# The first four units' key blocks of v are issued by GpSimd in its own queue, not by SyncE

## The chip, the cores and the metric

The kernel runs on one core of a Trainium2 chip. The metric is the device time of one execution in microseconds (us). TensorE is called PE, VectorE DVE, ScalarE ACT, GpSimd POOL and SyncE SP, as the profile does.

## What is computed

An attention over 2 batches, 8 heads, 768 positions and 64 dimensions, in float32, and behind it two dense layers of expert form. A query sees the keys less than 16 positions away, and besides one summary per block of 32 positions (the maximum of the block's keys, the mean of its values).

```
scores_l = scale * q @ k.T            # kept where |i - j| < 16
scores_s = scale * q @ k_sum.T + log(32)
a = softmax(concat(scores_l, scores_s))
x = a @ concat(v, v_sum)              # to [1536, 512]
x = relu(x @ w_in) ** 2 @ w_out       # 512 -> 2048 -> 512
h = x @ w_in2
out = (h * sigmoid(1.702 * h)) @ w_out2
```

## The kernel before

The 1536 tokens are twelve units of 128, units 0 to 5 in the first batch. For a unit, `scores` multiplies q by the keys of its two half windows and by the 24 summaries, and DVE adds the mask and finds the row's extreme (line 750). `softmax` takes the exponentials on ACT (line 765), adds a small number to the sums (line 769, here on POOL), inverts them on DVE (line 779) and multiplies (line 772, on DVE or on POOL). `tail` transposes the result on PE (line 802) and multiplies it by v (line 814). It then splits the product into a high and a low part, `xh` and `xl` (line 827), which the first layer's matmuls read (line 998). All matmuls of the layers are done three times, on high and low parts, to keep float32 accuracy.

For the product with v each unit has a tile `vw`: for each of its two halves (c = 0, 1) 96 rows of v around the half, the key block, and 24 rows of summaries. `load_vw` brings the key blocks with one DMA per half (line 509). A key block of 96 positions and 8 heads is 768 pieces of 64 numbers, 256 bytes each; the very first block has 80 positions, as the window begins before the text does. There are four such tiles (`vw_ring`). The summary rows are put into two of them by copies (line 521) and into the other two by DMAs that POOL issues (line 531).

The summaries of v need the whole of v: three loads of 512 KB into `kin` buffers (`load_long`, line 474, and `load_short`, line 481), whose blocks PE averages (line 576) before DVE and ACT copy the result to `vs` (line 364). There are three `kin` buffers, and the loads of k use them as well.

The order of the work is planned by the program before the kernel exists. A string of items, ORDER, names the steps of the attention (`v,0` is `load_vw(0)`, `h` a head step, `t` a tail, `w` the preparation of a weight block) in the order in which they are placed. `Plan.op` gives each step a start time from costs written beside it, and all steps are emitted by start time, so that each engine has one fixed list and works through it in order. `plan.dma` places a DMA on SP. `plan.fill` adds matmuls on the identity (line 1774, "warm") where PE would stand idle. DMAs of SP share eight semaphores in turn, so an issue can wait for the DMA eight before it.

```
def dma(self, moves, fn, reads=(), writes=()):
    return self.op("SP", 0.0, fn, reads, writes, moves=moves)
```

Of the kernel before, what the change touches and what calls it, by code (L numbers as in the profile page):

```python
# [39 lines left out]
LAST = (2,), (0, 1), (3,)  # L40
SHAKE = (14, 0.15)
WARM = (15.52, 6), (21.24, 5)
KEPT = 10
LOW3 = 7.4999 / 2.0 ** 32
LESS = 99.0
# [97 lines left out]
class Plan:  # L143
# [37 lines left out]
    def op(self, eng, dur, fn, reads=(), writes=(), after=(), port=False, moves=0.0):  # L181
        ready = self._ready(eng, self._deps(reads, writes, after)) + self._shaken()
        assert not any(b.dead for b, _ in (*reads, *writes))
        o = Op()
        o.eng, o.fn, o.seq, o.far = eng, fn, len(self.ops), eng == "SP"
        if eng == "SP":
            o.start = self._place(("SP",), max(ready, 0.8), self.ISSUE)
            self._take("SP", o.start, self.ISSUE)
            t = self._place(("DMA",), o.start + self.FLIGHT, moves)
            if t > o.start + self.FLIGHT:  # L190
                self.busy["SP"].remove((o.start, o.start + self.ISSUE))
                o.start = self._place(("SP",), t - self.FLIGHT, self.ISSUE)
                self._take("SP", o.start, self.ISSUE)
                t = self._place(("DMA",), o.start + self.FLIGHT, moves)
            self._take("DMA", t, moves)
            o.end = t + moves + self.LAND
        else:
            lines = (eng, "PORT") if port else (eng,)
            o.start = self._place(lines, ready, dur)
            for e in lines:  # L200
                self._take(e, o.start, dur)
            o.end = o.start + dur
        self.ops.append(o)
        for b, key in reads:
            b.ops.append(o)
            b.readers.setdefault(key, []).append(o)
        for b, key in writes:
            b.ops.append(o)
            b.writer[key] = o
            b.readers[key] = []  # L210
        return o
# [96 lines left out]
def kernel(  # L308
# [11 lines left out]
    nc = tc.nc  # L320
# [38 lines left out]
    plan = Plan()  # L359
# [135 lines left out]
    def load_vw(i):  # L495
        b, j = divmod(i, NB)
        assert vw_ring.k == i
        buf = vw_ring.take()
        rows = vs_rows[i % NV]
        for c in range(2):  # L500
            r0 = NSUM * (1 - c)
            s0 = j * P + c * HALF - EDGE
            lo, hi = max(s0, 0), min(s0 + WIN, S)
            if s0 < 0:
                op("POOL", 0.46, lambda c=c: nc.gpsimd.memset(buf.t[0:HALF, c, :], 0.0),
                   writes=[(buf, (c, "w")), (rows, c)])
            if s0 + WIN > S:
                op("POOL", 0.46, lambda c=c: nc.gpsimd.memset(buf.t[HALF:WIN, c, :], 0.0), writes=[(buf, (c, "w"))])
            plan.dma(1.0, lambda c=c, r0=r0, s0=s0, lo=lo, hi=hi: nc.sync.dma_start(
                out=buf.t[r0 + lo - s0:r0 + hi - s0, c, :].rearrange("p (h d) -> p h d", h=H),  # L510
                in_=v[b, :, lo:hi, :].rearrange("h p d -> p h d")), writes=[(buf, (c, "w"))])
        vw[i] = buf
# [1191 lines left out]
    def drain():  # L1704
        while pending:
            finish()

    todo = dict(
        K=load_kl, B=load_ks, T=t_kp, V=sum_v0, g=head_half, q=load_q, k=load_k, v=load_vw, tk=t_k, tq=t_q,
        h=head, t=tail, ps=put_vs, pk=put_ks, sv=sum_v, w=lambda f, z: prep(0, f, f % RING, (z,)),  # L1710
        m=lambda i: op("POOL", 1.6, lambda: make_mask(i), writes=[(consts, ("mask", i))]),
# [15 lines left out]
    if 0 in TWICE:  # L1727
        firsts = [int(item.split(",")[1]) for item in ORDER.split() if item[:2] == "w," and item[-2:] == ",0"]
        to_save.update({f for _, f in keep_w}, [f for f in firsts[::-1] if (0, f) not in keep_w][:KEPT])
    attn_ops = []  # L1730
# [44 lines left out]

    plan.fill(0.27, keep_warm, first_ops["acc3"], WARM)
    with tc.manual_schedule():
# [30 lines left out]
```

## Time and profile before

| | |
|---|---|
| median of 3 runs | 567.93 us (567.53 to 568.5) |
| the profiled execution | 568.08 us, span 566.4 us |
| PE busy | 560.2 us, 99% of the span |
| DVE, ACT, POOL busy | 495.6, 412.7, 41.8 us |
| granted TensorE clock | 1.00 |
| DMA | 120.26 MB, mean 212 GB/s |
| queue of SP (hardware), queue of POOL (software) | 104416 and 192 packets |

The profile is of one execution; its span is what the trace covers, and the 1.7 us between it and the time lie around it. Issuing a DMA is not counted as busy. A DMA has an issue on the engine that starts it, with a duration of its own, and a landing, counted from the issue until its semaphore is complete. A wait is put down to the event that came last.

### The profile page before, as it was taken

What the parts mean: (1) busy time and instruction counts of PE and PEld (TensorE: products, weight loads), DVE (VectorE), ACT (ScalarE), POOL (GpSimd) and SP (SyncE); (2) the same over time, 40 slices, a digit from 0 to 9 for tenths busy, and PEclk for the clock granted to TensorE, in tenths of its full rate; (3) what the DMA queues carried; (4) which work ended last, traced back from release to release, by engine and by line L of the source; (5) the groups of instructions that cost most, each with busy time, mean ns of one, the idle gap of its engine ahead of it and who ended that gap; (6) DMA issues with size and microseconds to landing.
All of it is one profiled execution on the core that took longest, in us unless ns stands there. A gap on an engine that the chain in (4) does not pass through costs nothing.

```text
span 566.4 us, 11027 instructions
## 1 busy us (share of the span) xinstructions
PE 560.2 (99%) x3838; PEld 481.3 (85%) x3838; DVE 495.6 (88%) x1110; ACT 412.7 (73%) x899; POOL 41.8 (7%) x112
## 2 busy tenths in 40 slices
PE   8999999999999999999999999999999999999997
PEld 8889988888878887888888888888888888899997
DVE  4788898888889899989999899998999999789974
ACT  4899889898896668777789757477366676677650
POOL 6143311211100000000000000000000000000000
PEclk9999999999999999999999999999999999999999
DMA  9999999886677864545558657576255555686723
GB/s 273 247 270 281 273 267 302 262 216 198 208 238 259 269 221 148 182 152 168 186 181 282 206 168 235 185 241 199 92 203 187 176 200 191 213 286 205 222 90 112
DMA packets 104663, 120.26 MB, mean 212 GB/s; under 512 B 28736, under 2 KB 72512, under 8 KB 104608
## 3 DMA queue, kind: packets, MB, share of 16 engines
q1 hardware_dynamic: 104416, 119.17, 67.1%
q0 software_dynamic: 192, 0.39, 0.4%
q8 instruction: 30, 0.49, 0.4%
q14 instruction: 25, 0.20, 0.1%
HBM read 86.64 MB, written 32.51 MB: 210 GB/s over the span
## 4 chain that ended last, share of the span: by engine, by line
PE 94%; SPq 1%; DMA 1%; DVE 1%; ACT 1%; issue 0%; DVEq 0%; ACTq 0%
PE acc L1440 14%; PE m L1440 12%; PE h L998 10%; PE acc L1053 8%; PE acc L1347 8%; PE acc L1345 7%; PE m L1345 5%; PE acc L998 5%; PE m L1347 4%; PE m L1055 4%; PE acc L1055 3%; PE h L1347 2%; PE h L1345 2%; PE m L802 2%; PE m L814 2%; PE m L998 1%
## 5 line engine op out<-in xcount | busy, mean ns | idle before, releaser
L963 DVE TENSOR_TENSOR w<-xw,w 128x512 fp32r<-128x512 f32 (+1 forms) x141 | 83.9, 609 | 2.7 <-ACT w L958 2.0
L958 ACT CAST w<-xw 128x512 fp32r<-128x512 f32 (+1 forms) x127 | 68.5, 552 | 23.0 <-DVE xw L932 15.9
L998 PE MATMUL h<-xh,w 128*128 128x512 f32 (+1 forms) x184 | 55.6, 364 | 0.0
L1440 PE MATMUL m<-top,w 128*128 128x512 f32 x210 | 53.5, 391 | 0.1
L932 DVE SCALAR_TENSOR_TENSOR xw<-raw,xw 128x512 uint32<-128x512 uint32 x67 | 45.8, 689 | 4.6 <-ACT raw L923 2.7
L923 ACT ACTIVATE raw<-raw 128x512 f32<-128x512 f32 x72 | 47.7, 679 | 1.0 <-DMA raw<-in_moe_w_in_dram 0.8
L1440 PEld LDWEIGHTS m<-top,w 128*128 128x128 f32 x210 | 38.7, 188 | 8.2 <-ACT r L363 0.5
L1440 PE MATMUL acc<-top,w 128*128 128x512 f32 x174 | 43.9, 390 | 0.0
L1053 PE MATMUL acc<-gh,w 128*128 128x512 f32 (+1 forms) x160 | 42.6, 353 | 0.0
L1440 PE MATMUL acc<-xh,w 128*128 128x512 f32 x124 | 42.1, 389 | 0.0
L1440 PEld LDWEIGHTS acc<-top,w 128*128 128x128 f32 x174 | 32.4, 188 | 6.5
L998 PEld LDWEIGHTS h<-xh,w 128*128 128x128 f32 x184 | 33.1, 189 | 5.6 <-issue 1.0
L765 ACT ACTIVATE sm<-sm,st 128x120 f32<-128x120 f32 x96 | 36.6, 385 | 0.2
L927 DVE TENSOR_SCALAR xw<-raw 128x512 uint32<-128x512 uint32 x67 | 29.1, 438 | 6.8 <-DMA raw<-in_moe_w_in_dram 5.4
L998 PE MATMUL h<-xl,w 128*128 128x512 f32 (+1 forms) x92 | 32.5, 353 | 0.0
L958 ACT CAST top<-gs 128x512 fp32r<-128x512 f32 x38 | 23.5, 618 | 11.3 <-DVE gs L947 3.0
L1053 PEld LDWEIGHTS acc<-gh,w 128*128 128x128 f32 x160 | 27.7, 189 | 4.4 <-issue 0.3
L963 DVE TENSOR_TENSOR top<-gs,top 128x512 fp32r<-128x512 f32 x41 | 27.9, 685 | 2.8 <-ACT top L958 2.6
L1347 PE MATMUL acc<-w,gh 128*128 128x256 f32 x136 | 28.0, 283 | 0.0
L1053 PE MATMUL acc<-gl,w 128*128 128x512 f32 (+1 forms) x80 | 27.8, 348 | 0.0
L1440 PEld LDWEIGHTS acc<-xh,w 128*128 128x128 f32 x124 | 23.3, 188 | 4.8
L998 PE MATMUL acc<-xh,w 128*128 128x512 f32 x80 | 26.1, 389 | 0.0
(300 smaller groups left out, 1501.6 us busy)
## 6 DMA issues: line engine op xcount, KB each, us to landing
raw<-in_moe_w_in_dram SPq DMA_DIRECT2D x36, 512.0 KB, 4.7
raw<-in_moe_w_out_dram SPq DMA_DIRECT2D x36, 512.0 KB, 4.6
w<-xw SPq DMA_DIRECT2D x50, 256.0 KB, 2.3
xw<-w SPq DMA_DIRECT2D x27, 256.0 KB, 2.8
w<-w SPq DMA_DIRECT2D x24, 256.0 KB, 2.8
r<-g SPq DMA_DIRECT2D x17, 256.0 KB, 3.7
vw<-in_v_dram SPq DMA_DIRECT2D x20, 192.0 KB, 4.7
g<-w SPq DMA_DIRECT2D x14, 256.0 KB, 2.0
```

The lines of the kernel that those rows point to most:

```text
L765: nc.scalar.activation(out=s.t[:, h, :], in_=s.t[:, h, :], func=AF.Exp, bias=st.t[:, 0, h:h + 1], scale=-1.0, accum_out=st.t[:, 1, h:h + 1])
L923: nc.scalar.activation(out=top, in_=top, func=AF.Prelu, scale=-(2.0 ** -80), alpha=-(2.0 ** -32))
L927: plan.soonest([("DVE", 0.36, True, lambda: nc.vector.tensor_scalar(out=x.t, in0=raw.t[:, :, 0], scalar1=29, scalar2=None, op0=ALU.logical ...
L932: op("DVE", 0.64, lambda: nc.vector.scalar_tensor_tensor(out=x.t, in0=raw.t[:, :, 1], scalar=3, in1=x.t, op0=ALU.logical_shift_left, op1=A ...
L958: plan.soonest([("ACT", 0.09 + 0.44 * fr, False, lambda: nc.scalar.copy(out=hi.t[:, hc], in_=src())), ("DVE", 0.05 + 0.4 * fr, True, lambd ...
L963: eng.tensor_tensor(out=lo.t[:, lc], in0=src(), in1=hi.t[:, hc].bitcast(F32), op=ALU.subtract)
L998: nc.tensor.matmul(hp.t[:, cols], lhsT=w.t[:, kc * P:(kc + 1) * P], rhs=x.t[:, kc, cols], start=(kc == 0 and n == 0), stop=(kc == KC - 1 a ...
L1053: nc.tensor.matmul(a.t[:, cols], lhsT=w.t[:, j * P:(j + 1) * P], rhs=g.t[:, cols], **st)
L1055: nc.tensor.matmul(a.t, lhsT=g.t[:, j * P:(j + 1) * P], rhs=w.t, **st)
L1345: nc.tensor.matmul(b.t, lhsT=w.t[:, x + j * P:x + j * P + P], rhs=g.t, **st)
L1347: nc.tensor.matmul(b.t[:, (j % 2) * CH:(j % 2) * CH + CH], lhsT=g.t[:, j * P:j * P + P], rhs=w.t[:, x:x + CH], **st)
L1440: nc.tensor.matmul(bank.t, lhsT=a, rhs=rhs(b, kh), start=(begin and k == 0 and n == 0), stop=(k == 1 and n == 2), skip_group_check=True)
```

## The change

A tuple names four units, and for them `load_vw` calls `dma_start` of GpSimd in place of that of SyncE. The plan is the same: it still counts the DMA as one of SP's, so start times and every other step stay, and the eight calls now stand in POOL's list at the places that their planned times give.

```
+BESIDE = 0, 1, 2, 3
...
+            queue = nc.gpsimd if i in BESIDE else nc.sync
-            plan.dma(1.0, lambda c=c, r0=r0, s0=s0, lo=lo, hi=hi: nc.sync.dma_start(
+            plan.dma(1.0, lambda c=c, r0=r0, s0=s0, lo=lo, hi=hi, queue=queue: queue.dma_start(
                 out=buf.t[r0 + lo - s0:r0 + hi - s0, c, :].rearrange("p (h d) -> p h d", h=H),
                 in_=v[b, :, lo:hi, :].rearrange("h p d -> p h d")), writes=[(buf, (c, "w"))])
```

The lines behind the first are one later in the changed kernel, and those from line 509 on two: line 509 becomes 511, 769 becomes 771. The lists of PE, DVE and ACT do not change.

POOL before, from the last of the copies that fill the windows of k's first units to the steps of unit 3's softmax (`st` and `sm` are the sums and the scores of a softmax):

```order
L662 COPY kw<-kw 128x5x16
L769 TENSOR_SCALAR st_344<-st_344 128x4
L769 TENSOR_SCALAR st_391<-st_391 128x4
L769 TENSOR_SCALAR st_344<-st_344 128x4
L521 COPY vw<-vs_451 24x512
...
L772 TENSOR_TENSOR sm_519<-sm_519,st_520 128x480
L678 MEMSET kw 128x4x16
L769 TENSOR_SCALAR st_520<-st_520 128x4
```

and the same stretch of POOL in the changed kernel:

```order
L664 COPY kw<-kw 128x5x16
L511 DMA vw<-in_v_dram 80x8x64
L511 DMA vw<-in_v_dram 96x8x64 x2
L771 TENSOR_SCALAR st_344<-st_344 128x4
L511 DMA vw<-in_v_dram 96x8x64 x2
L771 TENSOR_SCALAR st_391<-st_391 128x4
L511 DMA vw<-in_v_dram 96x8x64
L771 TENSOR_SCALAR st_344<-st_344 128x4
L523 COPY vw<-vs_451 24x512
...
L774 TENSOR_TENSOR sm_519<-sm_519,st_520 128x480
L511 DMA vw<-in_v_dram 96x8x64
L680 MEMSET kw 128x4x16
L511 DMA vw<-in_v_dram 96x8x64
L771 TENSOR_SCALAR st_520<-st_520 128x4
```

Six of the eight issues stand around the first two softmax steps, and two ahead of the sixth, that of unit 3's second half.

SP before, from the last loads of v for the summaries on (`kin_470` and `kin_526` are loads of k, `raw` a weight block):

```order
L481 DMA kin_339<-in_v_dram 128x8x128
L509 DMA vw<-in_v_dram 80x8x64
L509 DMA vw<-in_v_dram 96x8x64 x5
L449 DMA kin_470<-in_k_dram 128x4x128 x2
L449 DMA kin_526<-in_k_dram 128x4x128
L918 DMA raw_557<-in_moe_w_out_dram 128x1024
L449 DMA kin_526<-in_k_dram 128x4x128
L509 DMA vw<-in_v_dram 96x8x64 x2
L918 DMA raw_656<-in_moe_w_out_dram 128x1024
```

and in the changed kernel:

```order
L482 DMA kin_339<-in_v_dram 128x8x128
L450 DMA kin_470<-in_k_dram 128x4x128 x2
L450 DMA kin_526<-in_k_dram 128x4x128
L920 DMA raw_557<-in_moe_w_out_dram 128x1024
L450 DMA kin_526<-in_k_dram 128x4x128
L920 DMA raw_656<-in_moe_w_out_dram 128x1024
```

The loads of k now follow the last load of v directly; unit 4's key block is the first that SP still issues.

## Rows read from the trace of the kernel before

**Rows 1.** The page, part 1: busy us (share) and instructions of each engine.

```profile
PE 560.2 (99%) x3838; PEld 481.3 (85%) x3838; DVE 495.6 (88%) x1110; ACT 412.7 (73%) x899; POOL 41.8 (7%) x112
```

**Rows 2.** Windows: us, busy PE, PEld, DVE, ACT, POOL, clock, DMA share, GB/s.

```profile
15.00:20.00 5.00, 4.36 (x80) 3.95 (x76) 4.18 (x17) 3.98 (x10) 0.00 (x0) 1.00 1.11 332
...
50.00:170.00 120.00, 120.00 (x1085) 100.92 (x1083) 102.33 (x302) 105.74 (x277) 20.96 (x36) 1.00 0.83 248
```

**Rows 3.** The chain that ended last, 0 to 50: start us, us, what.

```profile
9.44 7.63 DMA qin<-in_q_dram
...
21.19 1.06 PE m L576 x16
...
24.19 0.28 DVE vs L364
...
30.27 0.65 PE m L802 x4
...
34.73 1.63 PE h L998 x12
...
41.48 1.08 PE acc L814 x32
```

**Rows 4.** Timeline, PE's weight loads: start us, us, what, [idle before <-releaser].

```profile
21.18 0.79 PEld L576 LDWEIGHTS m<-kin,band 128*24 128x24 f32 x16 [0.31 <-DMA kin<-in_v_dram]
```

**Rows 5.** Timeline of SP's DMA issues, first 60 us.

```profile
12.75 1.21 SPq L474 DMA_DIRECT2D kin<-in_v_dram  x2
...
15.20 9.23 SPq L509 DMA_DIRECT2D vw<-in_v_dram  x6
24.53 1.58 SPq L449 DMA_DIRECT2D kin<-in_k_dram  x3
...
27.91 1.91 SPq L509 DMA_DIRECT2D vw<-in_v_dram  x2
```

**Rows 6.** DMA queues, 19.6 to 21.2 us: packets, MB, share of 16 engines.

```profile
DMA packets 1017, 0.30 MB, mean 186 GB/s; under 512 B 879, under 2 KB 1017, under 8 KB 1017
...
q1 hardware_dynamic: 1017, 0.30, 99.1%
```

**Rows 7.** Timeline of POOL, first 60 us.

```profile
13.44 0.26 POOL L662 COPY kw<-kw 128x80 f32<-128x80 f32 x1
21.46 0.23 POOL L769 TENSOR_SCALAR st<-st 128x4 f32<-128x4 f32 x1 [7.77 <-ACT sm L765]
22.96 0.22 POOL L769 TENSOR_SCALAR st<-st 128x4 f32<-128x4 f32 x1 [1.28 <-ACT sm L765]
24.48 0.22 POOL L769 TENSOR_SCALAR st<-st 128x4 f32<-128x4 f32 x1 [1.29 <-ACT sm L765]
...
31.46 0.99 POOL L772 TENSOR_TENSOR sm<-sm,st 128x480 f32<-128x480 f32 x1 [0.17 <-DVE st L779]
...
33.16 0.22 POOL L769 TENSOR_SCALAR st<-st 128x4 f32<-128x4 f32 x1 [0.61 <-ACT sm L765]
```

**Rows 8.** Line 531, DMAs that POOL issues already: ns min/median/max, and landing.

```profile
L531 POOL DMA_DIRECT2D vw<-vs x4: 592/638/802, 25.9 to 101.8; - x4
...
DMA to landing us min/median/max: 4.1/5.6/7.4
```

**Rows 9.** Timeline of DVE, first 60 us.

```profile
24.19 0.28 DVE L364 COPY vs<-m 24x128 f32<-24x128 f32 x1 [1.53 <-PE m L576]
24.40 0.15 DVE L779 RECIPROCAL st<-st 128x4 f32<-128x4 f32 x1
...
25.64 0.17 DVE L779 RECIPROCAL st<-st 128x4 f32<-128x4 f32 x1
...
33.61 0.17 DVE L779 RECIPROCAL st<-st 128x4 f32<-128x4 f32 x1
33.70 0.66 DVE L827 TENSOR_TENSOR xl<-acc,xh 128x512 fp32r<-128x512 f32 x1
```

**Rows 10.** Timeline of PE, first 60 us: first use of xl.

```profile
34.89 0.28 PE L998 MATMUL h<-xl,w 128*128 128x256 f32 x1
```

## Prediction

> **What bounds the kernel now.** Read the engines' busy times first [rows 1]: TensorE is busy for 560.2 of 566.4 us. Then read stretches [rows 2]: from 50 to 170 us PE has no idle time at all, from 15 to 20 us it has 0.64 us. So nothing later in the run can be shortened by a change of queue, and little of a delay can be made up there. What the change can move is the moment at which PE comes into steady work. The chain of waits gives that moment [rows 3]: up to 17.1 us it hangs on the q load that was issued at 9.44 us, then on PE, then on v's sums on PE (line 576), which the copy of vs on DVE waits for at 24.19 us, then on DVE, and from 30.27 us on it stays on PE. At 34.73 us the first matmuls of the MoE layer start. A delay that still exists there goes to the end one for one.
>
> Two details decide. The second group of the v sums starts at 21.18 us behind a wait of 0.31 us for a v load [rows 4]; this is the place at which a slower load costs at once. And the softmax steps of line 769 on POOL feed DVE's reciprocals with little room [rows 7, 9]: the second ends at 23.18 and its reciprocal starts at 24.40, the third ends at 24.70 and is used at 25.64, the sixth ends at 33.38 and is used at 33.61.
>
> **What is removed from SP.** Eight issues go: six that hold SP from 15.20 to 24.43 us and two from 27.91 to 29.82 us [rows 5]. The k loads behind them now wait for the kin buffer that the first v sums read, free at about 21.2 us [rows 3], so they leave some 3.2 us sooner than at 24.53. I count this as nothing: what covers it is PE's and DVE's own order between 24 and 35 us, where the chain shows no load [rows 3]. If the cover failed it could only show in DVE's idle 1.53 us before the copy of vs [rows 9].
>
> **What is added on POOL.** Eight issues of 256-byte pieces: 640 pieces in the first, 768 in each other one. Three stand behind the copy that ends at 13.70, two between the first and the second softmax step, one between the second and third, two between the normalisation that ends at 32.45 and the sixth step [rows 7]. How long POOL needs for one, call it g, is not in the trace: the nearest rows are POOL's four issues of vs, 48 pieces each, median 0.638 us [rows 8]. Below, g is 0.64 if the number of pieces costs nothing; above it is 16 times that, 10.2 us, if every piece costs the same. I take 1.8 us: 1017 packets in 1.6 us at 99.1% of 16 engines are 25 ns per packet and engine [rows 6], so one such DMA (48 packets per engine) drains in 1.2 us, and I let the issue go at that pace on top of its 0.6. That lies near the lower row, since a regular pattern should not pay a full issue per piece. The Trainium skill, "DMA: Bandwidth & Descriptors", Anatomy of one DMA — SWDGE, goes further down: many descriptors can be emitted before their cost shows. By that sentence g is 0.64 and the sum below is 2.2 us; no run here shows it yet.
>
> Term 1, the transfers. Before, vw's packets stood behind the v loads in SP's queue. Now the first three DMAs are in a queue of their own from 13.70 us, beside the v loads issued from 12.75 us [rows 5], while the engines have no room (share 1.11 from 15 to 20 us [rows 2]). Their 2176 packets are 136 per engine, or 3.4 us at 25 ns. Bounds: 0 (they drain behind the v loads as before) to 3.4 us (all go ahead of the second v load). With g of 1.8 us the third is issued at 19.1 us, too late to get ahead; the first two are 88 packets per engine, **2.2 us**. The wait at 21.18 us has no slack, so they count in full. A delay of the q load that lands at 17.1 us by the first DMA (40 packets, at most 1.0 us) lies on the same chain ahead of it and is inside the 2.2. What speaks against is that POOL's own vs DMA took up to 7.4 us to land, against 4.1 at best [rows 8]: its queue gives way, too. The Trainium skill has in the same page, Queues, rings and completion order, that an engine goes round robin between queues packet by packet; by it the term would be the full 3.4 us, and the 7.4 us, where three packets per engine waited among SP's, fits that badly.
>
> Term 2, POOL's steps between 21 and 26 us. The first step may slip 0.5 us with the q load, to 22.2; two DMAs to 25.8; second step to 26.0; one DMA to 27.8; third step ends 28.0. With term 1 its reciprocal is due at 25.64 + 2.2 = 27.8. So **0.2 us** of it shows, nothing if g is below 1.7.
>
> Term 3, the last two issues. With 2.4 us of delay the normalisation ends at 34.85; two DMAs to 38.45; the sixth step ends at 38.7, and its reciprocal was due at 33.61 + 2.4 = 36.0. That is 2.7 late. Behind it stands line 827 on DVE, which ends at 34.36 and is first read at 34.89 [rows 9, 10]: 0.5 us of room. **2.2 us** remain. The key blocks themselves are just in time: with the longest landing, 7.4 us [rows 8], they are there at 45.9, and the tail that reads them, at 41.48 in the chain [rows 3], has slipped to 46.1.
>
> **Sum:** 2.2 + 0.2 + 2.2 = 4.6 us. The profiled execution took 568.08, within 0.15 of the median 567.93; from the median this gives **572.5 us**. Both ends of the terms: 0 transfers and g of 0.64 give 568 (two issues then take 1.3 us against 0.7 of gap before the sixth step, covered by 0.2 + 0.5 of room); above, it is open, see the second rival.
>
> **Rivals.** (a) *Nothing shows*: SP's queue keeps its share and g is near 0.64; 568.0. For it: the 7.4 us of landing [rows 8] and POOL's emptiness from 13.70 to 21.46 us [rows 7]. Against it: no slack at 21.18. (b) *POOL becomes the bound*: g is 3 us or more. Then the first three end at 22.7, the first step at 22.9, two more 28.9, second step 29.1, one 32.1, third step 32.4 against 25.64: 6.7 late. The normalisation ends at 39.2, two more 45.2, the sixth step 45.4 against 33.61: 11.8 late, less 0.5, so 579.2 us; above 2.5 us each further us of g adds 8. For it: 768 pieces against 48. Against it: nothing but the floor. (c) *Faster*: SP, free 3.2 us sooner, and a v load with no vw pieces crowding its tail let the third v sum end sooner. The chain then shortens by the idle time before the copy of vs, at most 1.53 us [rows 9]: 566.4. It decides when the v loads land more than 1.1 us sooner than now; the only wait for them that shows is 0.31 us [rows 4], which speaks against. (d) *It does nothing*: the listing shows the eight issues on POOL, so this has 1 in 100 and is held in (a).
>
> **Chances.** Measured times of this kernel differ by up to 0.2% without a cause, 1.1 us: no change is 566.8 to 569.1. Forecast (569.1 to 577) 0.56; (a) 0.18; (b) above 577, 0.20; (c) 0.06. So faster 0.06, no change 0.18, slower 0.76. The range leaves out about 0.04 below 567.4 and 0.13 above 580.0, where g passes 3 us. The forecast's own range is 569.1 to 577.
>
> **What would show it.** Right: line 511 on POOL in rows of 1.5 to 2.2 us; the second group of line 576 starting near 23.4 us; the third softmax step on POOL behind a DMA and not behind ACT; the first MoE matmul near 39.3 us; PE without idle afterwards. Wrong: rows of 0.6 to 0.8 us with line 576 unmoved (a); rows of 3 us and more with DVE's reciprocals waiting for POOL in every unit (b); the copy of vs before 23 us (c). A clock below 1.00 in the opening, where PE would now idle longer than before, would add a cost that no row here prices. If the delay at 34.7 us were not found again at the end, the first paragraph's reading would be wrong.

## The result and the profile after

The changed kernel takes **570.67 us** (median of 6 runs, 570.23 to 572.04) against 567.73 us before (6 runs in the same comparison, 567.38 to 568.62): ratio 1.0053, 95% interval 1.0039 to 1.0067. It is slower by 2.9 us; forecast were 572.5 us and a range of 567.4 to 580.0. The profiled execution took 570.4 us with a span of 568.6, 2.2 us more than before.

Part 1 of the page, busy us by engine, answers to [rows 1]. POOL has eight instructions and 7.4 us more; the eight issues, which are counted here, make 6.5 of them:

```profile
PE 559.6 (98%) x3838; PEld 481.0 (85%) x3838; DVE 496.7 (87%) x1110; ACT 412.6 (73%) x899; POOL 49.2 (9%) x120
```

The windows, with columns as in [rows 2]:

```profile
15.00:20.00 5.00, 5.00 (x97) 4.55 (x98) 4.89 (x25) 4.58 (x15) 2.53 (x3) 1.00 1.14 345
20.00:25.00 5.00, 2.12 (x28) 1.72 (x20) 1.39 (x8) 3.33 (x18) 3.04 (x6) 1.00 1.13 220
...
50.00:170.00 120.00, 120.00 (x1116) 101.48 (x1115) 102.71 (x302) 105.25 (x277) 21.82 (x36) 1.00 0.84 247
```

The same stretch of the opening in the kernel before, which [rows 2] leave out:

```profile
20.00:25.00 5.00, 4.96 (x85) 3.91 (x78) 3.16 (x21) 4.88 (x26) 0.67 (x3) 1.00 0.72 150
```

The steady part is as it was, and the loss stands in the opening: from 20 to 25 us PE works for 2.12 us of 5, where it worked for 4.96. The clock is at 2.4 GHz throughout in this execution. The chain that ended last, start us, us, what:

```profile
13.69 11.31 DMA kin<-in_v_dram
25.00 0.04 issue
25.04 0.68 PE m L578 x16
25.72 0.02 issue
25.75 0.28 DVE vs L365
...
31.83 0.65 PE m L804 x4
...
34.43 0.60 issue
35.03 0.34 PE acc L816 x4
...
37.12 1.62 PE h L1000 x12
```

Set against [rows 3], the copy of vs is 1.56 us later (25.75 against 24.19), the transpose behind it still 1.56 (31.83 against 30.27), and the first MoE matmul 2.39 (37.12 against 34.73). In between stands a second loss: PE waits 0.60 us in the middle of the second product with v, and nothing that the profile shows releases it ("issue"); the product is 0.83 us longer in all. The 2.39 us are found again at the end as 2.2.

The chain begins with the *third* v load, issued at 13.69 us and landed after 11.31. PE's timeline says the same, with the idle time and its releaser in brackets:

```profile
19.02 1.79 PE L578 MATMUL m<-kin,band 128*24 128x128 f32 x32
25.04 0.64 PE L578 MATMUL m<-kin,band 128*24 128x128 f32 x16 [2.92 <-DMA kin<-in_v_dram]
```

The first two v sums run without a break, where [rows 4] had a wait of 0.31 us before the second; it is the third that waits. SP's queue (answering to [rows 5]) and POOL's timeline ([rows 7]):

```profile
20.12 1.47 SPq L450 DMA_DIRECT2D kin<-in_k_dram  x3
21.69 0.48 SPq L920 DMA_DIRECT2D raw<-in_moe_w_out_dram  x1
```

```profile
15.16 2.53 POOL L511 DMA_DIRECT2D vw<-in_v_dram  x3 [1.82 <-issue]
20.40 0.22 POOL L771 TENSOR_SCALAR st<-st 128x4 f32<-128x4 f32 x1 [2.71 <-ACT sm L767]
20.68 1.58 POOL L511 DMA_DIRECT2D vw<-in_v_dram  x2
22.33 0.22 POOL L771 TENSOR_SCALAR st<-st 128x4 f32<-128x4 f32 x1
22.60 0.81 POOL L511 DMA_DIRECT2D vw<-in_v_dram  x1
23.48 0.22 POOL L771 TENSOR_SCALAR st<-st 128x4 f32<-128x4 f32 x1
```

```profile
L511 POOL DMA_DIRECT2D vw<-in_v_dram x8: 776/807/947, 15.2 to 34.9; - x8
```

POOL's issue of 768 pieces takes 0.81 us (ns min/median/max in the last row), against 0.638 for 48 pieces [rows 8]: sixteen times the pieces cost 0.17 us. SP's k loads leave 4.4 us sooner. What the engines carry from 20 to 22 us is in the view of DMA queues (packets, MB, share of 16 engines):

```profile
q0 software_dynamic: 128, 0.38, 101.6%
q1 hardware_dynamic: 59, 0.03, 8.7%
```

[rows 6] had SP's queue alone there. POOL's queue moves packets of 4096 bytes (sixteen of the 256-byte pieces in one); the third v load goes in packets of 512 bytes. A landing is sixteen increments of a semaphore, so it has sixteen parts, presumably one for each DMA engine. The trace's semaphore events give, for the third v load:

| run | 8th part, us | 15th part | 16th part (landing) |
|---|---|---|---|
| before | 20.31 | 21.68 | 22.80 |
| change | 20.34 | 22.30 | 25.00 |

The 8th part is no later, and none of the first fifteen is more than 0.8 us later. The last part lags already before the change, and under POOL's packets it loses 2.2 us more.

### The profile page after: what moved, and what is told of

Read it like the earlier page. It is cut to its first block, busy times and chain, and to the rows that moved or that the text cites. A ratio compares the mean times of both kernels' runs of the same rounds, so it can differ in the third digit from the quotient of the medians.

```text
span 568.6 us, 11033 instructions
## 1 busy us (share of the span) xinstructions
PE 559.6 (98%) x3838; PEld 481.0 (85%) x3838; DVE 496.7 (87%) x1110; ACT 412.6 (73%) x899; POOL 49.2 (9%) x120
## 4 chain that ended last, share of the span: by engine, by line
PE 94%; DMA 3%; DVE 1%; ACT 1%; SPq 0%; issue 0%; DVEq 0%; ACTq 0%
PE acc L1442 14%; PE m L1442 12%; PE h L1000 10%; PE acc L1349 8%; PE acc L1055 8%; PE acc L1347 7%; PE m L1347 5%; PE acc L1000 5%; PE m L1349 4%; PE m L1057 4%; PE acc L1057 3%; PE h L1349 2%; DMA kin<-in_v_dram 2%; PE h L1347 2%; PE m L804 2%; PE m L816 2%
```

## Experiments

Theory A: the key blocks' packets in POOL's queue hold up the third v load. Theory B: the time that POOL needs for the issues delays its softmax steps. The expectation for units 0 to 2 names a third, C: the loads of SP, which now leave sooner, collide with PE's fetch of instructions (in the last run C stands for something else, the clock). Edits are shown against the changed kernel; the lines that carry AT into the plan are shown once.

**The kernel before, once more.** No edit.

> The kernel before, once more, for a second trace. Open point: in the trace of the change the q load of 9.1 us and the first two v loads took 6.4, 5.8 and 6.9 us to land, in the trace of before 7.6, 6.5 and 7.9, and PE reached the fill ahead of the third v sum at 20.74 in place of 22.17 us. If this is a gain of the change (eight fewer issues behind them in SP's queue), the control shows the longer landings again, within 0.3 us, and the fill at 22.0 to 22.3. If it is scatter between executions, the control may show either.

Measured: 569.25 us in one execution, the profiled one; 23 other executions of the same kernel in this comparison have the median 567.83 (566.86 to 568.98). The copy of vs starts at 23.91 us. But PE's timeline has a wait that the first profile of this kernel did not have:

```profile
31.56 1.03 PE L814 MATMUL acc<-pT,vw 120*64 120x64 f32 x28
33.85 0.34 PE L814 MATMUL acc<-pT,vw 120*64 120x64 f32 x4 [1.26 <-issue]
```

So the "issue" wait in the second tail comes and goes in the unchanged kernel, too. Of the 2.39 us in the profile of the change, only the 1.56 at the copy of vs is left for the change, and that is a difference to one profile; the copy scatters, as the run of unit 3 below shows.

The open point of the expectation is scatter as well. The second v load took 8.4 us to land here (20.86) and 8.0 before (21.14), against 6.9 in the change; but with unit 3 alone on POOL, where SP's list is that of before up to 28 us, it took 7.0. In both profiles of before the chain to the copy of vs leads from the second load, and the third sum does not wait.

**Units 0 to 2 alone.**

```
-BESIDE = 0, 1, 2, 3
+BESIDE = 0, 1, 2
```

> Only the key blocks of units 0 to 2 on POOL, those of unit 3 on SP. Theory A (POOL's queue takes the DMA engines from the third v load, and PE then loses another 0.8 us at its tail because the two late issues of unit 3 crowd the engines as an instruction block is fetched): third v load lands near 25 us, copy of vs near 25.7, and the 0.8 us of idle PE in the second tail is gone: 1.6 us over before. Theory B (POOL's own time: softmax steps wait behind issues): the late pair is away, the early six hide; the same time as before. Theory C (the loads of SP, now some 4 us sooner, collide with PE's fetch): as the change, 2.4 to 3 us over before, with PE's idle time in the tail.

Measured: 571.1 us (569.98 to 572.65, 6 runs), ratio 1.0057 (1.0041 to 1.0073). The third v sum waits 1.83 us for its load, which lands at 24.33, and the copy of vs is at 25.08. The whole loss is there without the two late issues. The 1.6 us that A put on it are too few, though, and the wait in the second tail, which A had gone, is there with 0.60 us, as theory C has it. C is not needed for that wait, since the control has a longer one with SP's loads in their old places; it is not excluded either.

**Unit 3 alone.**

```
-BESIDE = 0, 1, 2, 3
+BESIDE = 3,
```

> Only unit 3's two key blocks on POOL; the first six stay on SP. Theory A: the third v load lands near 22.8 as before, copy of vs at 24.2; over before by 0.8 us if the two late issues make PE wait, as A says. Theory B: the sixth softmax step waits for two issues of 0.8 us, 0.7 us late against its reciprocal's 0.2 us of room: 0.5 to 0.8 us over before. Theory C: SP's order is nearly that of before up to 28 us, so the same time as before.

Measured: 568.05 us (567.34 to 571.28, 11 runs), ratio 1.001 (0.9997 to 1.0023): no difference that these runs can tell. DVE does wait for POOL's sixth step behind the two issues:

```profile
33.24 0.18 DVE L781 RECIPROCAL st<-st 128x4 f32<-128x4 f32 x1 [0.75 <-POOL st L771]
```

and this comes through: the chain that ended last runs over POOL's two issues and xl, and PE's first matmul on xl starts 0.53 us behind the one on xh, where before it was 0.22 (34.67 and 34.89):

```profile
33.52 0.39 PE L1000 MATMUL h<-xh,w 128*128 128x256 f32 x1
34.05 0.39 PE L1000 MATMUL h<-xl,w 128*128 128x256 f32 x1
```

The late pair cost some 0.3 us in this profile. It does not look later than [rows 3] because the third v load landed at 22.01 us and the copy of vs started at 22.88, 1.31 us sooner than in the first profile of before, with the first six key blocks in SP's queue as there: that is scatter. For the late pair, then, theory B keeps 0.3 us, in line with the 0.1% of the eleven runs. For the early six the profile of the change speaks against it: POOL's third step ends at 23.70 us, and DVE takes it up at 27.19.

**All key blocks with SP, but the first six behind two k loads.** AT sets planned start times by step number; 114 and 115 are unit 0's key blocks, 123 and 124 unit 1's, 125 and 126 unit 2's, 149 and 150 the k loads.

```
-BESIDE = 0, 1, 2, 3
+BESIDE = ()
+AT = {149: 18.6, 150: 18.61, 123: 18.71, 124: 18.72, 114: 19.71, 115: 19.72}
...
+    for o in plan.ops:
+        o.start = AT.get(o.seq, o.start)
```

> All key blocks on SP, but the six of units 0 to 2 behind the first two k loads instead of ahead of them, so that no vw packet can run beside v loads. Theory A: the third v load lands at 21 to 22 us at the latest, the third v sum starts right after PE's fill, and the copy of vs comes up to 1.4 us sooner than at 24.19: 0.5 to 1.4 us under before. Rival: vw's packets behind the v loads in one queue never hurt them (the landing of 22.8 us was due to something else): copy of vs at 24.2, the same time as before, or slower by up to 1 us, as the tail of unit 1 waits for its key block.

Measured: 569.01 us (568.48 to 570.4, 11 runs), ratio 1.0023 (1.0014 to 1.0031). With nothing beside it the third v load lands at 21.37 us and the copy of vs starts at 23.02, 1.17 us sooner than before. This shows no gain from moving the key blocks: the third sum waits for its load neither here nor before, the second load was 1.17 us sooner too (19.97 against 21.14), and the run of unit 3 had the copy at 22.88 with the key blocks in their old places. So the rival of the expectation stands. What makes the time longer is at 35.78 us, where DVE waits 2.27 us for a weight block:

```profile
35.78 0.43 DVE L930 TENSOR_SCALAR xw<-raw 128x512 uint32<-128x512 uint32 x1 [2.27 <-DMA raw<-in_moe_w_out_dram]
```

**The six issues later on POOL**, behind its first two softmax steps.

```
+AT = {123: 23.05, 124: 23.06, 114: 24.57, 115: 27.0, 125: 28.38, 126: 28.39}
```

> All eight issues stay on POOL, but the first six stand behind the first two softmax steps of POOL, so that none of their packets can run before about 22 us, when the third v load of the kernel before has landed. Theory A (the key blocks cost only because POOL's queue crowds out the third v load, which shares its stretch with them): the third v sum starts without a wait for its load at 22.2 to 23.5 us, the copy of vs at 22.9 to 24.2 us against 25.75 in the change, and the time is 566.9 to 568.6 us, no slower than the kernel before by more than 0.2%. Theory B (key blocks in POOL's queue cost wherever they stand, by POOL's time for the issues or by a late landing): the copy of vs may be early, but the products with v then wait for their key blocks or the reciprocals for POOL's steps, and the time stays at 570 to 571 us.

Measured: 574.75 us (573.47 to 576.18, 4 runs), ratio 1.0116 (1.0097 to 1.0135). The copy of vs is early, at 23.49 us, as A says, but the time is worse than either theory has it; of the two, B's text described the wait. The key blocks take a median of 10.6 us to land, and the first product with v waits for them:

```profile
30.83 0.48 PE L817 MATMUL acc<-pT,vw 120*64 120x64 f32 x4 [2.41 <-POOL st L772]
34.90 1.76 PE L817 MATMUL acc<-pT,vw 120*64 120x64 f32 x28 [3.58 <-DMA vw<-in_v_dram]
```

After these waits the clock stands at 0.54 and 0.50 (1.2 GHz) from 30 to 40 us. The run moved the collision from the v load to the key blocks and separates nothing.

**The third v load in POOL's queue too**, ahead of the key blocks.

```
+        queue = nc.sync if src is k else nc.gpsimd
-        plan.dma(0.85 if len(gs) == 1 else 1.78, lambda: nc.sync.dma_start(
+        plan.dma(0.85 if len(gs) == 1 else 1.78, lambda: queue.dma_start(
```

> The change, and the third v load goes into POOL's queue as well, ahead of the key blocks, so that the two no longer stand in different queues. Theory A1 (a queue of SP with packets of 512 bytes loses against POOL's queue with packets of some 3 KB, because the engines take turns packet by packet): the third load goes ahead of the key blocks and has packets as large, so it lands by 20 to 22 us, the third v sum does not wait for it, the copy of vs is at 22.5 to 23.5 us, and the time is 566.5 to 568.6 us. Theory A2 (all that counts is how many bytes are moved in the stretch, whatever the queue): the load lands no sooner than in the change, 25 us, and the time is about 570.5 us.

Measured: 571.32 us (569.69 to 574.53, 6 runs), ratio 1.0068 (1.0043 to 1.0093). The load lands at 22.67 us, so A2's 25 us is out, and A1's 20 to 22 is missed, too; the third v sum does not wait, and the copy of vs is at 23.41. The time did not follow. Now a key block that POOL issued behind its first softmax step is late for the first product, and the "issue" wait in the second tail is 1.30 us:

```profile
29.24 1.03 PE L817 MATMUL acc<-pT,vw 120*64 120x64 f32 x28 [0.64 <-DMA vw<-in_v_dram]
```

**The third v load alone in POOL's queue**, all key blocks with SP (the edit above, and BESIDE empty).

> The kernel before, with the third v load alone in POOL's queue; all key blocks stay in SP's queue in their old places. Now the roles are swapped: by theory A1 the third v load (large packets) wins against the key blocks (packets of 256 bytes) and takes 4 to 6.5 us from issue to landing, against 8.8 us in the kernel before and 11.3 us in the change; while it runs, POOL's queue has the larger share of the engines by far. By theory A2 it takes 8 us or more, as the key blocks are in the same stretch. The time is not what this run is for: 566.5 to 569.3 us either way.

Measured: 8.7 us from issue to landing, not the 4 to 6.5 of A1; the time of this one execution is 569.79. The first packet moves at 17.90 us, 2.7 us after the issue began, and the parts are spread from there on (8th at 21.42, 15th at 22.28, 16th at 23.85). Large packets alone do not make a load quick.

**The six early key blocks in ACT's queue.**

```
-BESIDE = 0, 1, 2, 3
+BESIDE = 0, 1, 2
...
-            queue = nc.gpsimd if i in BESIDE else nc.sync
+            queue = nc.scalar if i in BESIDE else nc.sync
```

> The six early key blocks go into ACT's hardware queue (unit 3's two stay with SP), where the issues stand between ACT's copies and exponentials. Theory A1: in a hardware queue their packets hold 256 bytes against the third v load's 512, so taking turns by packet leaves that load the larger share in bytes: it lands within 9 us of its issue and the third v sum waits for it by less than 0.7 us, against 2.92 in the change. Theory A2: as many bytes run beside the load as in the change, it takes some 11 us and the third v sum waits 1.8 to 3 us. ACT itself will be late by its issues, so the time is not what this run is for; some 570 to 576 us.

Measured: nearly the same bytes, in packets of 256 bytes, beside the same load (0.51 MB up to 22.9 us, 0.54 in the change; in both the first three key blocks). It lands at 22.90 us, 9.1 after its issue and between the 22.80 and 22.99 of the two profiles of before, and the third v sum does not wait, though this queue fills the engines from 20 to 22 us as POOL's did:

```profile
q10 hardware_dynamic: 1250, 0.31, 115.2%
q1 hardware_dynamic: 88, 0.04, 10.8%
```

So neither a queue of their own nor the bytes beside the load suffice for the delay; here it took POOL's queue, with its large packets. Which of the two it is, the queue or the size of its packets, no run separates. (The time of the one execution, 573.85 us, is that of ACT, which was late by its issues: PE waits 4.09 us for a normalisation at 30.75.)

The last four ask what a dose does, what remained when the load was on time, and what part the scatter has.

**All six in one row ahead of POOL's first softmax step**, the third v load with SP.

```
+AT = {125: 20.5, 126: 20.51, 123: 20.3, 124: 20.31, 114: 20.1, 115: 20.11}
```

> The change, with all six early key blocks issued by POOL in one row before its first softmax step; the third v load stays with SP. If POOL's key blocks hold up the last packets of the third v load (theory A), twice as many of them now stand beside it: it lands at 25.0 us or later (25 to 27), while most of its sixteen parts are complete by 21 us as in the change, and the third v sum waits 2.9 us or more. If the late landing came from something else, such as the instruction block that one engine carried at 22.33 us, it does not grow with the number of key blocks: 23 to 25 us.

Measured: 575.87 us in one execution, span 574.1. The load lands at 28.70 us, later than the 25 to 27 expected:

```profile
28.74 1.07 PE L579 MATMUL m<-kin,band 128*24 128x128 f32 x16 [4.02 <-DMA kin<-in_v_dram]
```

Fifteen of its parts are complete at 22.41 us, as in the change; the sixteenth takes 6.3 us longer. The second v load is late here, too (22.30), and its sum waits 1.34 us. The delay grows with the number of key blocks in POOL's queue, which an instruction block in the way, the rival of the expectation, would not make it do. This is the plainest run for theory A.

**The same row of six, with the third v load ahead of it in POOL's queue** (both edits).

> As in the run before with the third v load ahead of the key blocks in POOL's queue, but all six early key blocks are issued in one row behind it, before POOL's first softmax step. Their issues take about 0.79 us each and the load's 1.14, so from 15.4 us they end at 21.3, some 0.4 us behind the time at which the first step was free to start (20.9). Theory D (with the third v load on time, what was left of the loss came from key blocks that POOL issues only behind its softmax steps and that land 7 to 8 us later, just when the first product with v needs them): the wait of 0.64 us for vw goes, the last early key block lands by 27 us, and the time falls from 571.3 to between 567.5 and 569.3. Theory E (POOL's queue costs through what runs beside it, late instruction blocks and low clock among it, wherever the key blocks stand): the wait for vw goes too, but the time stays above 570.

Measured: 568.54 us (568.24 to 573.35, 11 runs), ratio 1.0025 (1.0008 to 1.0041). No product waits for a key block, although the last early one lands at 29.28 and not by 27; the load lands at 23.57 and the third v sum waits 0.60 us; the first MoE matmul is at 35.14, 0.41 us behind [rows 3]. Theory D has the time right (567.5 to 569.3), theory E (above 570) does not: what was left of the loss with the load on time came for the most part from the key blocks that POOL issued behind its steps. Of the change's 0.5% half is gone with the eight key blocks still on POOL. It took both edits: the load ahead in the queue alone measured 1.0068. And it does not beat the kernel before.

**The changed kernel once more.** No edit.

> The changed kernel once more, for a second profile. Theory A: the third v load lands at 24.3 to 25.5 us again and the copy of vs starts 1 us or more later than in the kernel before (23.9 and 24.2 us in two profiles). The idle time of PE inside the second tail (0.60 us) may be anything from 0 to 1.3, as it differs between two profiles of the kernel before. Rival: the copy of vs is as early as in the kernel before, so its lateness was scatter of one execution.

Measured: 571.86 us in one execution, span 570.1. The load lands at 25.66, the copy of vs is at 26.41. There is no "issue" wait in the second tail; in its place the clock falls after the 2.81 us of waiting, for part of the time to 1.2 GHz, so that the windows show means between the two levels (columns as above):

```profile
20.00:25.00 5.00, 2.88 (x36) 2.20 (x32) 1.81 (x12) 3.75 (x20) 3.04 (x6) 1.00 1.11 215
25.00:30.00 5.00, 4.30 (x56) 3.71 (x59) 3.34 (x15) 3.14 (x11) 1.20 (x2) 0.71 1.10 245
30.00:35.00 5.00, 5.00 (x100) 4.48 (x99) 3.73 (x22) 3.54 (x15) 1.83 (x5) 0.95 1.14 270
```

The copy is 2.22 us later than in [rows 3] and the first MoE matmul 3.67 (38.40): the clock cost some 1.45 us, and the span is longer by 3.7.

**More work for PE in the wait.**

```
-WARM = (15.52, 6), (21.24, 5)
+WARM = (15.52, 6), (21.24, 15)
```

> The change, with fifteen in place of five matmuls on the identity in front of the third v sum: PE works for 4.1 us there in place of 1.4, about as long as it had to wait, and its instructions behind are shifted against their blocks of 256. Theory C (in part of the executions the 2.9 us of idle time cost clock: three of the six runs of the change had a mean granted clock of 0.996, 0.4% of 568 us or some 2 us of half speed): no run is below 0.999 and the median falls to 569.3 to 570.2. Rival (the clock has no part, all is the late load): 570.3 to 571.2, as the change.

Measured: 570.86 us (570.79 to 571.63, 5 runs), ratio 1.0053 (1.004 to 1.0067). All five runs have a mean clock of 0.999 or 1.00, so the first half of theory C holds, but the median is no lower. The profile has the "issue" wait, 1.29 us, and in another place:

```profile
33.47 0.45 PE L816 MATMUL acc<-pT,vw 120*64 120x64 f32 x8
35.22 0.92 PE L816 MATMUL acc<-pT,vw 120*64 120x64 f32 x24 [1.29 <-issue]
```

It stands behind the 8th matmul of the tail, not behind the 28th: 20 matmuls with their 20 weight loads earlier, as many instructions as the ten added fills (two matmuls and two loads each) put in front. The wait belongs to a place in PE's list of instructions. It goes with a block of instructions that is fetched late: packets of 16,384 bytes run in a queue of instructions (kind "instruction") at 29.26 us in the first profile of before, which has no wait, and at 31.20, 32.46 and 32.64 in the control, the change and this run, which have one. In these three PE goes on 1.4 to 1.5 us after the end of that packet; in the first profile of before it had ended 1.4 us ahead of the tail. What makes a fetch late was not tried.

**All profiles together.** The third v load with SP, by what ran beside it:

| key blocks beside the third v load | landing, us | copy of vs, us |
|---|---|---|
| none (behind k loads; later on POOL) | 21.37, 21.84 | 23.02, 23.49 |
| SP's queue (before, control, unit 3 alone) | 22.80, 22.99, 22.01 | 24.19, 23.91, 22.88 |
| ACT's queue, three | 22.90 | 23.64 |
| POOL's queue, three (change twice, units 0 to 2, more work for PE) | 25.00, 25.66, 24.33, 25.07 | 25.75, 26.41, 25.08, 25.82 |
| POOL's queue, six | 28.70 | 29.88 |

POOL's queue stands apart from the scatter of the others. At the copy of vs it costs 2.1 us in the mean (0.9 to 3.5) against SP's queue; the 1.56 of the first pair of profiles is one draw from that. The rest of the 2.9 us, some 0.8, differs from execution to execution, and no run assigns it.

## Why the prediction came out as it did

- **What bounds the kernel**: right. What the first MoE matmul loses is found at the end: +2.39 and +2.2 us in the change, +3.67 and +3.7 in its second profile, +0.41 and +0.6 in the run with both edits.
- **Removed from SP, counted as nothing**: right for the time. The k loads left 4.4 us sooner, not 3.2, and nothing was gained. Whether the third load gains by having no vw packets beside it is not shown: it landed at 21.37 and 21.84 us without them, at 22.01 to 22.99 with them in SP's queue, and no third sum waited in any of these.
- **The price of an issue, g**: wrong. It is 0.81 us, not 1.8, near the lower bound; the pieces are nearly free. The sentence of the Trainium skill that was weighed there ("DMA: Bandwidth & Descriptors", Anatomy of one DMA — SWDGE: many descriptors before their cost shows) agrees with this row. The 2.2 us given there as the sum by that sentence do not follow from the prediction's own terms: with issues of 0.64 us all three early DMAs are out by 15.6 us, and term 1 would be its upper bound, 3.4.
- **Term 1, the transfers, 2.2 us**: right that the packets in a queue of their own hold up a v load; the load and the way were not. It named the second v load and a wait at 21.18 us without slack; that load was not late at all (19.70 against 21.14), the third one was. The row on which this rested, a wait of 0.31 us, told which load was nearest to the edge before, not which one the new packets would meet: they start at 19.04 us, 3.9 us after the first issue, when the second load lacked three of its sixteen parts and the third all of them. The load lands 2.2 us later (25.00 against 22.80), of which 1.56 shows at the copy of vs; 2.2 us in the second profile. That this is the term's figure is luck: it counted 88 packets of 256 bytes per engine at 25 ns, all ahead of the load. In fact sixteen pieces went in one packet, and fifteen of the load's parts were hardly later; the last one was.
- The rule weighed there, that an engine goes round robin between queues by packets (the Trainium skill, "DMA: Bandwidth & Descriptors", Queues, rings and completion order), was set aside for the 7.4 us of landing in [rows 8]. The runs speak for it as far as they go: beside packets of 4096 bytes the load's last part is late, beside as many bytes in packets of 256 it is not. It does not explain why the load alone in POOL's queue took 8.7 us.
- **Term 2, POOL's steps, 0.2 us**: nothing, as it said for g below 1.7. The third step ends at 23.70 us, and DVE takes it up at 27.19.
- **Term 3, the last two issues, 2.2 us**: wrong in size. It came from g. With 0.81 the sixth step makes DVE wait 0.73 us, and the 0.5 us of room ahead of the first use of xl takes most of that. In the change nothing of it reaches PE (37.05 and 37.27 for xh and xl); some 0.3 us do where the loads are early: alone, unit 3's issues measure 1.001 (0.9997 to 1.0023).
- **Sum**: 4.6 us forecast, 2.9 measured; the sign is that of term 1. Of the signs of being right only one came, the third softmax step behind a DMA, and it cost nothing. The first MoE matmul was at 37.12 and 38.40 us, not near 39.3. What stands in the place of terms 2 and 3 differs from execution to execution: a late instruction block (0.60 us in one profile) or a low clock (some 1.45 us in the other). The prediction named the second as a cost that no row could price.
- **Rivals**: (a) had g right and the outcome wrong; its signs, rows of 0.6 to 0.8 us with the v sums unmoved, came half true. (b) needed 3 us per issue. (c), a copy of vs before 23 us, came in the run of unit 3 alone (22.88), by scatter; without key blocks beside the loads the copy was at 23.02 and 23.49, with no gain at the end.

## What to carry to other kernels

Before a DMA goes to another queue, list the loads that will be *in flight* when its first packet moves, not when it is issued, and look at the load among them whose last part already lags; that part sets the landing. If a transfer must go to POOL's queue, let the load that it may not hold up go ahead of it in the same queue, and issue the transfer early: here both together took the ratio from 1.0053 to 1.0025, the first alone did not (1.0068). And take a second profile of the unchanged kernel before reading differences of 1 us: the second tail moved by 1.26 us on its own, and the copy of vs by 1.3 with the same loads ahead of it.

## What was not expected of the hardware

- The last of the sixteen parts of the third v load lagged behind the fifteenth: by 0.4 to 1.5 us in the profiles without POOL's packets beside it, by 2.5 to 4.3 under three key blocks in POOL's queue, by 6.3 under six. The fifteenth was at 21.4 to 22.6 us in the profiles with POOL's packets and at 20.7 to 21.7 in the others.
- The first packet of POOL's queue moved 1.9 to 4.1 us after the issue began (the load and key blocks in one queue: 15.42 to 17.35; the change: 15.16 to 19.04; the six later issues: 22.97 to 27.03), so an early place in POOL's list is not an early transfer.
- The clock did not answer alike to like idle time: 2.92 us of waiting left it at 1.00 in one profile of the change, 2.81 us took it to 0.71 of full speed over the next 5 us in the other. With PE kept busy in that wait five runs of five had a mean of 0.999 or more.
